# The bias of a norm as four one-element operations, two float16 scratch buffers, and a later weight split

## The chip, the cores and the metric

The kernel runs on one core of one Trainium2 chip. The metric is the device time of one launch in microseconds (us). Before the change the median of 3 runs is 1232.11 us (1230.1 to 1235.2).

The engines of a core work side by side, each through a queue of its own, in order: PE multiplies matrices (PEld loads its stationary operand), DVE does element-wise work on 128 lanes, ACT does activations, copies and sums along a row, POOL does element-wise work in SBUF, and SP issues the DMAs. SBUF is the working memory, PSUM holds what PE writes.

## The reference

Eight batches of 4224 positions with 192 channels. First a dynamic convolution, in which each position and each of 8 heads has its own 7 taps, passed through a softmax. Then, with its output as x, a Fourier mixing, a normalisation and a two-layer network:

```
w = softmax(weight_gen, axis=-1)                    # (8, 4224, 8 heads, 7 taps)
x[b,s,h] = sum_k w[b,s,h,k] * x_pad[b, s+k, h]      # 24 channels to a head
u   = x + real(fft(fft(x, axis=seq), axis=channel))
un  = (u - mean(u)) / sqrt(var(u) + 1e-6)           # over the 192 channels
out = u + relu(un @ w_ch1) @ w_ch2                  # 192 -> 768 -> 192
```

The weights w_ch1 and w_ch2 arrive as 64-bit words. The kernel turns them into 32-bit floats on DVE.

## The kernel before, in words

A batch is 4224 = 128 x 33 positions: 128 partitions and 33 rows of 192 channels. The 33 rows are worked in nine groups, g = 0 to 7 with four rows and g = 8 with one. Per batch b there are these steps:

- conv(b): the softmax of the taps (L271 to L277), and then for each group the products of taps and inputs on DVE (`pr`, L389), which POOL adds up seven to a sum (`u`, L398). POOL folds the sum (`sm`, L410 and L412), PE transforms it along 128 positions (`pg`, L417), ACT and DVE combine the result (L422 to L427), and it goes to DRAM (`g_d`). In batch 0 some sums are made on PE (`pa`), and in batch 1 the products of the first two groups are made on POOL (L387).
- transform(b): `g` is read back, PE transforms it along the 33 rows (`pp`, L456), ACT copies it to `pq`.
- mix(b, g): PE transforms a group along the channels (`eo`, L485); DVE combines (L491, L492) and adds to `u` (L494, L495).
- norm(b, g): the mean and the variance of each of the group's T = 4 rows (one for g = 8). In five early groups ("quick") DVE computes them (L515, L516). In all others ACT sums a row (L521) and the squares of its deviation (L525). Both of these activations write their full result to a tile `junk` that nobody reads; only the accumulated sum is kept, in `st`. Then `rs[:,0]` = 1/sqrt(var + eps) by a square root on ACT (L527) and a reciprocal on DVE (L528), and the bias `rs[:,1]` = -mean * rs[:,0] on DVE in one operation on all T columns (L529). ACT applies scale and bias row by row (`un`, L532), and copies the result to float16 (`hl`, L536). POOL (DVE in the quick groups) computes the float16 remainder (L538, L540), and a DMA transposes both into `ht` (L543).
- mlp(n), n counting the groups of all batches: PE computes `ph` from `ht` and the high and low float16 halves of the first weights (30 matmuls, L568). ACT applies the relu (L574, L578), DVE computes the remainder of the float16 rounding (L579), and PE multiplies group n-1 with the second weights (`po`, L595). DVE scales this and adds it to `u` (L602), and a DMA writes it out.

The second weights exist in two forms. The first nine groups (`F32_GROUPS = 9`, all of batch 0) use the 32-bit `w2f`; all later ones use the float16 halves `w2h` and `w2l` and the scale `isc`. `split_w2` makes the halves: a largest exponent over all of `w2f` on DVE (L174, L175, L177), spread over the partitions by two small matmuls on PE into `ph` banks (L180, L183) with DVE work between them (L181, L184, L186, L188), then three L213, one L255 and three L214 on DVE. Before the change it is emitted at the very start of `rest()`, the stream that also carries conv(1), and may stand no earlier than behind the first matmul group of mlp(0).

The order on each engine is not written out by hand. The steps are generators with a start and an end place; `run()` interleaves them by place, and the framework then orders the instructions of each engine by its own estimate of their times and of when their inputs are ready. `issue_after` and `behind` set the earliest place of a piece. A change of one instruction's kind can therefore move others.

A tile from a pool with `bufs=1` is one buffer that each new use waits for; with `bufs=2` two uses can overlap.

Of the kernel before, what the change touches and what calls it, by code (L numbers as in the profile page):

```python
# [10 lines left out]
F16 = mybir.dt.float16  # L11
F32 = mybir.dt.float32
I32 = mybir.dt.int32
AF = mybir.ActivationFunctionType
ALU = mybir.AluOpType
# [4 lines left out]
P = 128  # L20
# [9 lines left out]
QUICK = 3  # L30
EARLY = 7.4
HELD = 7.0
PP_AT = 4.4
MIX_STEP = 0.8
PE_SUMS = {(0, 0), (0, 1), (0, 3), (0, 5), (0, 7)}
# [51 lines left out]
def tile_dynconv_fnet_mlp(  # L87
# [12 lines left out]
    nc = tc.nc  # L100
    B, D = x.shape[0], x.shape[3]
# [9 lines left out]
    sb = ctx.enter_context(tc.tile_pool(name="sb", bufs=2))  # L111
# [361 lines left out]
    last_product, last_fold, last_gt, last_g2, last_pp = {}, {}, {}, {}, {}  # L473
# [3 lines left out]
    def mix(b, g):  # L477

        u = us[b, g]
        J = 2 if g < NC else 1  # L480
        eo = pst("fft", 2, [P, 2, 2, DH], F32, f"eo_{b}_{g}")
        for e in range(2):
            for j in range(J):
                r = 2 * g + 1 + j if g < NC else 0
                nc.tensor.matmul(eo[:, e, j, :], lhsT=pq[0:DH, e, r, r:r + P], rhs=cs_sb[:, e, :],  # L485
                                 start=True, stop=True)
                yield 0.1 * (J * e + j + 1)
        if g < NC:
            ot = sb.tile([P, 2, DH], F32, tag="ot", name=f"ot_{b}_{g}", bufs=2)
            nc.scalar.copy(ot, eo[:, 1])  # L490
            nc.vector.tensor_tensor(out=eo[:, 1, ::-1, :], in0=eo[:, 0], in1=ot, op=ALU.subtract)  # L491
            nc.vector.tensor_tensor(out=eo[:, 0], in0=eo[:, 0], in1=ot, op=ALU.add)  # L492
            sv = eo.rearrange("p s j d -> p (s j) d")
            nc.vector.tensor_tensor(out=u[:, :, 0:DH], in0=u[:, :, 0:DH], in1=sv, op=ALU.add)  # L494
            nc.vector.tensor_tensor(out=u[:, :, DH:D], in0=u[:, :, DH:D], in1=sv[:, ::-1, DH - 2:0:-1], op=ALU.add)  # L495
        else:
            low, high = u[:, 0, 0:DH], u[:, 0, DH:D]
            for e, op in ((0, ALU.add), (1, ALU.subtract)):
                nc.vector.tensor_tensor(out=low, in0=low, in1=eo[:, e, 0], op=ALU.add)
                nc.vector.tensor_tensor(out=high, in0=high, in1=eo[:, e, 0, DH - 2:0:-1], op=op)  # L500
        yield 2.0

    def norm(b, g):

        T = min(4, N2 - 4 * g)
        u = uv = us[b, g]
        st = sb.tile([P, 4, 2], F32, tag="st", name=f"st_{b}_{g}", bufs=2)
        rs = sb.tile([P, 3, 4], F32, tag="rs", name=f"rs_{b}_{g}", bufs=2)
        junk = sb.tile([P, D], F32, tag="junk", name=f"junk_{b}_{g}", bufs=1)
        un = sb.tile([P, 4, D], F32, tag="un", name=f"un_{b}_{g}", bufs=1)  # L510
        quick = NG * b + g < QUICK or (b == 1 and g < 2)
        if quick:
            bn = sb.tile([P, 4, 6], F32, tag="bn", name=f"bn_{b}_{g}", bufs=2)
            for t in range(T):
                nc.vector.bn_stats(out=bn[:, t, :], in_=uv[:, t, :])  # L515
                last_bn[b, g] = nc.vector.bn_aggr(out=st[:, t, :], in_=bn[:, t, :])  # L516
            nc.scalar.activation(rs[:, 0, 0:T], st[:, 0:T, 1], AF.Sqrt, bias=eps_t)
            neg = -1.0
        else:
            for t in range(T):  # L520
                nc.scalar.activation(junk, uv[:, t, :], AF.Identity, accum_out=st[:, t, 0:1])  # L521
            neg = -1.0 / D
            nc.scalar.mul(rs[:, 2, 0:T], st[:, 0:T, 0], neg)
            for t in range(T):
                nc.scalar.activation(junk, uv[:, t, :], AF.Square, bias=rs[:, 2, t:t + 1],  # L525
                                     accum_out=st[:, t, 1:2])
            nc.scalar.activation(rs[:, 0, 0:T], st[:, 0:T, 1], AF.Sqrt, bias=eps_t, scale=1.0 / D)  # L527
        nc.vector.reciprocal(out=rs[:, 0, 0:T], in_=rs[:, 0, 0:T])  # L528
        nc.vector.scalar_tensor_tensor(out=rs[:, 1, 0:T], in0=st[:, 0:T, 0], scalar=neg, in1=rs[:, 0, 0:T],  # L529
                                       op0=ALU.mult, op1=ALU.mult)  # L530
        for t in range(T):
            nc.scalar.activation(un[:, t, :], uv[:, t, :], AF.Identity,  # L532
                                 bias=rs[:, 1, t:t + 1], scale=rs[:, 0, t:t + 1])
        yield 0.5
        hl = sb.tile([P, 4, 2 * D], F16, tag="hl", name=f"hl_{b}_{g}", bufs=2)
        nc.scalar.copy(hl[:, 0:T, 0:D], un[:, 0:T, :])  # L536
        lo_eng = nc.vector if quick else nc.gpsimd
        lo_eng.tensor_tensor(out=hl[:, 0:T, 2 * P:3 * P], in0=un[:, 0:T, 0:P],  # L538
                                in1=hl[:, 0:T, 0:P], op=ALU.subtract)
        last_lo[NG * b + g] = lo_eng.tensor_tensor(out=hl[:, 0:T, D:2 * P], in0=un[:, 0:T, P:D],  # L540
                                in1=hl[:, 0:T, P:D], op=ALU.subtract)
        ht = sb.tile([P, 4, 3, P], F16, tag="ht", name=f"ht_{b}_{g}", bufs=3)
        nc.sync.dma_start(ht[:, 0:T].rearrange("p t q m -> p (t q) m"),  # L543
                          hl[:, 0:T, :].rearrange("p t d -> p (t d)"), transpose=True)
        state[b, g] = (us.pop((b, g)), ht)
        yield 2.0
# [65 lines left out]
    def add(start, end, gen):  # L612
        streams.append([start, start, end, len(streams), gen])
# [13 lines left out]
    def behind(ins, gen):  # L627

        while True:
            with tc.issue_after(ins):  # L630
                at = next(gen, None)
            if at is None:
                return
            yield at

    def next_conv(b):
        yield from behind((last_gt if b == 2 else last_product)[b - 1].ins, conv(b))

    last_word, last_split, last_lo, last_bn, last_ph, scales = [], [], {}, {}, {}, []
# [4 lines left out]
    def queue(ins, *calls):  # L644
        with tc.issue_after(ins):
            for f, arg in calls:
                f(arg)
# [4 lines left out]
    conv1 = conv(1)  # L652
# [4 lines left out]
    for g in range(QUICK):  # L657
        add(0.0, 1.0, behind((last_word if g else last_split)[-1].ins, mix(0, g)))
        run()
        add(0.0, 1.0, norm(0, g))  # L660
        run()
        queue(last_bn[0, g].ins, (prep_w2, g))
# [1 line left out]
        queue(last_lo[QUICK - 1].ins, (prep_w2, i))  # L664

    def rest():
        with tc.issue_after(last_ph[0].ins):
            queue(last_lo[QUICK - 1].ins, (split_w2, None))
        yield 0.0
        yield from behind(last_ph[0].ins, behind(last_lo[QUICK - 1].ins, behind(last_g2[0].ins, conv1)))  # L670

    def held_mlp(n):
        gen = mlp(n)
        for at in gen:
            yield at
            if n + at >= HELD:
                break
        yield from behind(last_pp[1].ins, gen)

    for n in range(total + 1):  # L680
        add(n, n + 1.0, held_mlp(n) if n == int(HELD) else mlp(n))
    free_at = 1.0
    for b in range(B):
        t0 = NG * b
        pp_at, mix_at, step = (NG - HELD + 0.6, NG - HELD, 0.6) if b == 1 else (PP_AT, 3.0, MIX_STEP)
        if b > 0:
            add(free_at, t0 - pp_at, next_conv(b) if b > 1 else rest())
            add(t0 - pp_at, t0 - mix_at, transform(b))
            free_at = t0 - pp_at
        for g in range(NG):  # L690
            if b > 0 or g >= QUICK:
                at = t0 - mix_at + step * g
                add(at, at + step, mix(b, g))
                add(max(at + step, t0 + g - 2.0), t0 + g - 1.0, norm(b, g))
# [38 lines left out]
```

## Time and profile before

| | |
|---|---|
| median of 3 runs | 1232.11 us |
| the profiled execution, its own time | 1232.47 us |
| its span from the first to the last instruction | 1230.7 us |
| mean granted clock of PE | 0.963 |
| busy: PE, DVE, POOL, ACT | 1098.7, 1059.0, 867.8, 784.9 us |
| L529 (the bias), 72 instructions on DVE | 70.3 us, shortest 144 ns, median 540 ns, longest 5158 ns |
| L521 and L525 (`junk`), 488 on ACT, with their accumulator reads | 198.5 and 92.6 us |

Times in the profile are those of one execution. A busy time is the time in which an instruction of that engine was under way, waiting inside an instruction included. Rows of a view by windows give start and end of the window, its length, and then the busy time of each engine with the number of its instructions, the granted clock of PE as a share of full speed, the busy share of the DMA engines and GB/s. In a timeline a row gives start, duration, engine, line, operation and tiles; in the view by source line a row gives the count, and the shortest, median and longest duration in ns.

### The profile page before, as it was taken

To read this page: it belongs to the slowest core of one execution; us is meant where nothing else is said; L and a number is where in the kernel's file an instruction comes from. 1 tells how busy PE (TensorE), PEld (TensorE's weight loads), DVE (VectorE), ACT (ScalarE), POOL (GpSimd) and SP (SyncE) were. 2 spreads that over 40 slices of the span, in tenths; PEclk is the share of its full clock that TensorE was granted. 3 is DMA by queue.
4 is the path that set the end of the run, shared out by engine and by line. 5 is a ranking of instruction groups with operands and counts; after the bars stand their busy time and mean duration, and the time that the engine had idled before them with its cause. 6 is when DMAs were issued, how large, how long until landed. Compare 5 with 4: busy or idle time off the path is not lost.

```text
span 1230.7 us, 23500 instructions
## 1 busy us (share of the span) xinstructions
PE 1098.7 (89%) x8382; PEld 826.1 (67%) x8382; DVE 1059.0 (86%) x1849; ACT 784.9 (64%) x2353; POOL 867.8 (71%) x686
## 2 busy tenths in 40 slices
PE   5765698998899949999898989998999999999998
PEld 3435466777666827677577766787677776777777
DVE  7999899589999999999998999999989997355543
ACT  1015775263795578858785589657984589479822
POOL 4869478859895989699877988698959898002100
PEclk9986699999999969999999999999999999999999
DMA  8234124722366144633374145623453123512221
GB/s 306 84 109 144 26 59 106 196 77 69 100 170 139 61 97 98 178 95 94 83 190 116 49 110 154 158 66 99 125 134 91 53 68 78 129 43 69 57 64 43
DMA packets 156502, 128.71 MB, mean 105 GB/s; under 512 B 108571, under 2 KB 133088, under 8 KB 156384
## 3 DMA queue, kind: packets, MB, share of 16 engines
q1 hardware_dynamic: 156384, 127.21, 38.4%
q8 instruction: 66, 1.08, 0.4%
q14 instruction: 52, 0.43, 0.1%
HBM read 61.46 MB, written 39.37 MB: 82 GB/s over the span
## 4 chain that ended last, share of the span: by engine, by line
DVE 40%; PE 39%; ACT 7%; DMA 6%; issue 5%; POOL 2%; SPq 1%; DVEq 0%; ACTq 0%; POOLq 0%
PE ph L568 16%; PE po L595 14%; DVE pr L389 14%; DVE hh L579 6%; PE pp L456 5%; DVE rs L529 4%; DMA g<-g_d 2%; DVE u L602 2%; DVE u L389 2%; DMA g_d<-gt 2%; DVE u L494 2%; DVE u L495 2%; PE pg L417 1%; ACT hh L578 1%; PE eo L485 1%
## 5 line engine op out<-in xcount | busy, mean ns | idle before, releaser
L398 POOL TENSOR_TENSOR u<-u,pr 128x768 f32<-128x768 f32 (+1 forms) x395 | 654.8, 1681 | 92.9 <-DVE pr L389 78.3
L568 PE MATMUL ph<-ht,w1h 128*128 128x512 f16 (+1 forms) x1296 | 400.9, 366 | 28.8 <-DVE hh L579 13.5
L595 PE MATMUL po<-w2h,hh 128*128 128x192 f16 x2772 | 398.5, 247 | 11.8 <-DVE u L602 8.9
L595 PEld LDWEIGHTS <-hh 128*128 128x128 f16 x4158 | 356.4, 98 | 73.4 <-issue 13.1
L389 DVE TENSOR_TENSOR pr<-x_sb,wp 128x768 f32<-128x768 f32 (+1 forms) x420 | 357.1, 875 | 12.1 <-POOL u L398 8.1
L595 PE MATMUL po<-w2l,hh 128*128 128x192 f16 x1386 | 336.3, 247 | 0.0
L579 DVE SCALAR_TENSOR_TENSOR hh<-ph,hh 128x512 f16<-128x512 f32 (+1 forms) x378 | 238.5, 639 | 107.3 <-ACT hh L578 106.2
L568 PE MATMUL ph<-ht,w1l 128*128 128x512 f16 (+1 forms) x864 | 312.8, 366 | 0.0
L578 ACT ACTIVATE hh<-ph 128x512 f16<-128x512 f32 (+1 forms) x378 | 207.6, 554 | 125.9 <-PE ph L568 125.0
L538 POOL TENSOR_TENSOR hl<-un,hl 128x512 f16<-128x512 f32 (+1 forms) x67 | 72.7, 1085 | 190.1 <-ACT hl L536 126.6
L568 PEld LDWEIGHTS <-w1h 128*128 128x128 f16 x1296 | 127.2, 100 | 97.6 <-issue 5.8
L532 ACT ACTIVATE un<-u,rs 128x192 f32<-128x192 f32 x264 | 123.6, 537 | 60.1 <-DVE rs L529 52.1
L568 PEld LDWEIGHTS <-w1l 128*128 128x128 f16 x864 | 85.4, 99 | 85.4 <-issue 36.3
L525 ACT ACTIVATE junk<-u,rs 128x192 f32<-128x192 f32 x244 | 110.6, 453 | 4.6
L521 ACT ACTIVATE junk<-u 128x192 f32<-128x192 f32 x244 | 87.9, 360 | 23.1 <-DVE u L495 18.3
L485 PE MATMUL eo<-cs_sb,pq 97*128 97x97 f32 x544 | 82.7, 286 | 21.8 <-DVE u L495 20.6
L485 PEld LDWEIGHTS eo<-cs_sb,pq 97*128 97x128 f32 x544 | 77.4, 203 | 29.0 <-issue 12.7
L460 ACT COPY pq<-pp 97x204 f32<-97x204 f32 (+1 forms) x96 | 46.4, 484 | 65.2 <-PE pp L456 63.2
L595 PE MATMUL po<-w2f,hh 128*128 128x192 f32 x396 | 72.9, 330 | 3.3 <-DVE u L602 2.9
L602 DVE SCALAR_TENSOR_TENSOR u<-po,isc,u 128x384 f32<-128x384 f32 (+1 forms) x119 | 68.5, 596 | 7.9 <-PE po L595 7.5
L417 PE MATMUL pg<-sm,f_sb 128*128 128x192 f32 x256 | 56.4, 345 | 21.1 <-POOL sm L412 13.6
L595 PEld LDWEIGHTS po<-w2f,hh 128*128 128x128 f32 x396 | 66.5, 191 | 9.2 <-DVE u L602 3.7
(101 smaller groups left out, 1331.2 us busy)
## 6 DMA issues: line engine op xcount, KB each, us to landing
out_dram<-u SPq DMA_DIRECT2D x64, 384.0 KB
x_sb<-in_x_dram SPq DMA_DIRECT2D x48, 384.0 KB
g<-g_d SPq DMA_DIRECT2D x40, 336.0 KB
x_sb<-in_x_dram SPq DMA_DIRECT2D x8, 864.0 KB
g_d<-gt SPq DMA_DIRECT2D x32, 195.0 KB
g_d<-gt SPq DMA_DIRECT2D x32, 189.0 KB
w<-in_weight_gen_dram SPq DMA_DIRECT2D x6, 924.0 KB
x_sb<-in_x_dram SPq DMA_DIRECT2D x8, 672.0 KB
```

The lines of the kernel that those rows point to most:

```text
L389: last_product[b] = nc.vector.tensor_tensor(out=dst, in0=rows, in1=wk, op=ALU.mult)
L398: adder.tensor_tensor(out=u, in0=u, in1=pr, op=ALU.add)
L485: nc.tensor.matmul(eo[:, e, j, :], lhsT=pq[0:DH, e, r, r:r + P], rhs=cs_sb[:, e, :], start=True, stop=True)
L521: nc.scalar.activation(junk, uv[:, t, :], AF.Identity, accum_out=st[:, t, 0:1])
L525: nc.scalar.activation(junk, uv[:, t, :], AF.Square, bias=rs[:, 2, t:t + 1], accum_out=st[:, t, 1:2])
L532: nc.scalar.activation(un[:, t, :], uv[:, t, :], AF.Identity, bias=rs[:, 1, t:t + 1], scale=rs[:, 0, t:t + 1])
L538: lo_eng.tensor_tensor(out=hl[:, 0:T, 2 * P:3 * P], in0=un[:, 0:T, 0:P], in1=hl[:, 0:T, 0:P], op=ALU.subtract)
L568: last_ph[n] = nc.tensor.matmul(ph[:, 0:T], lhsT=wt[:, cs_], rhs=ht[:, 0:T, blk], start=(i == 0), stop=(i == len(terms) - 1))
L578: nc.scalar.activation(a[:, 0:T], ph[:, 0:T], AF.Relu)
L579: nc.vector.scalar_tensor_tensor(out=l[:, 0:T], in0=ph[:, 0:T], scalar=0.0, in1=a[:, 0:T], op0=ALU.max, op1=ALU.subtract)
L595: nc.tensor.matmul(po[jj][:, s, :], lhsT=hx[:, t], rhs=wx[:, c2, :], start=(c2 == 0 and i == 0), stop=(c2 == NH - 1 and i == nt - 1))
L602: nc.vector.scalar_tensor_tensor(out=lt, in0=po[jj][:, 0:m], scalar=scales[0][:, 1:2] if NG * lb + lg < F32_GROUPS else isc, in1=lt, op0=A ...
```

## The change

Three things. (1) The bias of the norm, one SCALAR_TENSOR_TENSOR on 128 x T elements, becomes T operations TENSOR_SCALAR on 128 x 1 elements: the mean is the only streamed tensor, and 1/sqrt comes in as a scalar per partition. The arithmetic is the same. (2) `junk` becomes float16 in two buffers, of the same bytes together as the one float32 buffer. (3) `split_w2` leaves the start of `rest()` and gets a stream of its own, `late_split()`, at place 6.0, not before the last matmul of mlp(5) and not before the latest product of conv(1) emitted by then.

```diff
+SPLIT = 5
...
     # in norm(b, g)
-        junk = sb.tile([P, D], F32, tag="junk", name=f"junk_{b}_{g}", bufs=1)
+        junk = sb.tile([P, D], F16, tag="junk", name=f"junk_{b}_{g}", bufs=2)
...
-        nc.vector.scalar_tensor_tensor(out=rs[:, 1, 0:T], in0=st[:, 0:T, 0], scalar=neg, in1=rs[:, 0, 0:T],
-                                       op0=ALU.mult, op1=ALU.mult)
+        for t in range(T):
+            nc.vector.tensor_scalar(out=rs[:, 1, t:t + 1], in0=st[:, t, 0:1], scalar1=rs[:, 0, t:t + 1],
+                                    scalar2=neg, op0=ALU.mult, op1=ALU.mult)
...
     def rest():
-        with tc.issue_after(last_ph[0].ins):
-            queue(last_lo[QUICK - 1].ins, (split_w2, None))
+        yield from behind(last_ph[0].ins, behind(last_lo[QUICK - 1].ins, behind(last_g2[0].ins, conv1)))
+
+    def late_split():
         yield 0.0
-        yield from behind(last_ph[0].ins, behind(last_lo[QUICK - 1].ins, behind(last_g2[0].ins, conv1)))
+        with tc.issue_after(last_ph[SPLIT].ins):
+            queue(last_product[1].ins, (split_w2, None))
+        yield 1.0
...
+    add(SPLIT + 1.0, SPLIT + 1.5, late_split())
```

The changed program has more instructions on DVE alone: 264 TENSOR_SCALAR stand for 72 SCALAR_TENSOR_TENSOR. All other instructions are the same on every engine, but their order differs in many places. Three of them follow, before and then changed. In the changed kernel the line numbers from L34 on are one higher, and from L532 on two.

The first place is DVE in the norms of groups 3 and 4 of batch 0, where the second softmax of conv(1) and the first step of `split_w2` (`ex_w20` to `ex_w22`, `mx_w2`) stand:

```order
L528 RECIPROCAL rs_0_3_991<-rs_0_3_991 128x4
L272 TENSOR_TENSOR w_1_624<-w_1_624,wp_1_623 128x1344
L529 SCALAR_TENSOR_TENSOR rs_0_3_991<-st_0_3_990,rs_0_3_991 128x4
L275 TENSOR_REDUCE wp_1_623<-w_1_624 128x192
L276 TENSOR_SCALAR wp_1_623<-wp_1_623 128x192
L277 RECIPROCAL wp_1_623<-wp_1_623 128x192
L174 TENSOR_SCALAR ex_w20_1013<-w2f_87 128x384
L174 TENSOR_SCALAR ex_w21_1016<-w2f_87 128x384
L174 TENSOR_SCALAR ex_w22_1019<-w2f_87 128x384
L528 RECIPROCAL rs_0_4_1151<-rs_0_4_1151 128x4
```

```order
L529 RECIPROCAL rs_0_3_1000<-rs_0_3_1000 128x4
L273 TENSOR_TENSOR w_1_624<-w_1_624,wp_1_623 128x1344
L531 TENSOR_SCALAR rs_0_3_1000<-st_0_3_999,rs_0_3_1000 128x1 x4
L529 RECIPROCAL rs_0_4_1134<-rs_0_4_1134 128x4
L531 TENSOR_SCALAR rs_0_4_1134<-st_0_4_1133,rs_0_4_1134 128x1 x4
L276 TENSOR_REDUCE wp_1_623<-w_1_624 128x192
L277 TENSOR_SCALAR wp_1_623<-wp_1_623 128x192
L278 RECIPROCAL wp_1_623<-wp_1_623 128x192
L349 TENSOR_TENSOR wp_1_623<-w_1_624,wp_1_623 128x224
L390 TENSOR_TENSOR u_1_2_1191<-x_sb_66,wp_1_623 128x768
```

The steps of the split are gone from here, the bias stands as four operations without anything between them, and the products of conv(1) follow the softmax directly.

The second place is DVE at the end of conv(1), between the last combinations of batch 1 (`gt_1_8`) and the softmax of conv(2):

```order
L426 TENSOR_TENSOR gt_1_8_1860<-pg_1_8_1858,up_1_8_1862 128x95
L427 TENSOR_TENSOR gt_1_8_1860<-pg_1_8_1858,up_1_8_1862 128x95
L271 TENSOR_REDUCE wp_2_1876<-w_2_1877 128x264
L272 TENSOR_TENSOR w_2_1877<-w_2_1877,wp_2_1876 128x1848
L275 TENSOR_REDUCE wp_2_1876<-w_2_1877 128x264
L602 SCALAR_TENSOR_TENSOR u_0_5_397<-po_0_5_0_1780,sc_w1_717,u_0_5_397 128x384
```

```order
L427 TENSOR_TENSOR gt_1_8_1884<-pg_1_8_1882,up_1_8_1886 128x95
L428 TENSOR_TENSOR gt_1_8_1884<-pg_1_8_1882,up_1_8_1886 128x95
L272 TENSOR_REDUCE wp_2_1900<-w_2_1901 128x264
L182 TENSOR_REDUCE m2_w2_1791<-mr_w2_1792 1x1
L273 TENSOR_TENSOR w_2_1901<-w_2_1901,wp_2_1900 128x1848
L604 SCALAR_TENSOR_TENSOR u_0_5_397<-po_0_5_0_1775,sc_w1_717,u_0_5_397 128x384
L604 SCALAR_TENSOR_TENSOR u_0_5_397<-po_0_5_1_1776,sc_w1_717,u_0_5_397 128x384
L185 TENSOR_SCALAR m2_w2_1791<-me_w2_1795 128x1
L187 TENSOR_SCALAR sc_w2_1798<-m2_w2_1791 128x1
L189 TENSOR_SCALAR sc_w2_1798<-m2_w2_1791 128x1
L214 TENSOR_SCALAR w2h_85<-w2f_87,sc_w2_1798 128x384 x3
L256 TENSOR_TENSOR isc_88<-sc_w1_717,sc_w2_1798 128x1
```

The split now stands here; its exponents (L175, L176, L178) lie a few rows ahead and its three L215 three rows behind, around the sum of the softmax (L276). L182 waits for a small matmul of PE, and the softmax of conv(2) is queued behind it.

The third place is ACT at the turn from batch 1 to batch 2, in the norms of the groups (2, 0) and (2, 1):

```order
L527 ACTIVATE rs_2_0_3866<-st_2_0_3865,eps_t_79 128x4
L521 ACTIVATE junk_2_1_4074,st_2_1_4072<-u_2_1_2100 128x192 x4
L523 ACTIVATE rs_2_1_4073<-st_2_1_4072 128x4
L525 ACTIVATE junk_2_1_4074,st_2_1_4072<-u_2_1_2100,rs_2_1_4073 128x192 x2
L422 COPY gt_3_2_4006<-pg_3_2_4003 128x4
L424 COPY up_3_2_4008<-pg_3_2_4003 128x190
L525 ACTIVATE junk_2_1_4074,st_2_1_4072<-u_2_1_2100,rs_2_1_4073 128x192 x2
L527 ACTIVATE rs_2_1_4073<-st_2_1_4072,eps_t_79 128x4
L532 ACTIVATE un_2_0_3868<-u_2_0_1888,rs_2_0_3866 128x192 x4
```

```order
L528 ACTIVATE rs_2_0_3914<-st_2_0_3913,eps_t_79 128x4
L491 COPY ot_2_2_4099<-eo_2_2_4034 128x194
L580 ACTIVATE hh_1_8_3_4235<-ph_1_8_3_4222 128x128
L580 ACTIVATE hh_1_8_4_4266<-ph_1_8_4_4254 128x128
L522 ACTIVATE junk_2_1_4125,st_2_1_4123<-u_2_1_2124 128x192
L534 ACTIVATE un_2_0_3916<-u_2_0_1912,rs_2_0_3914 128x192 x3
L522 ACTIVATE junk_2_1_4125,st_2_1_4123<-u_2_1_2124 128x192
L534 ACTIVATE un_2_0_3916<-u_2_0_1912,rs_2_0_3914 128x192
```

Before, the rows of group (2, 0) are normalised behind all eight sums of group (2, 1); now behind one of them.

## The prediction

> **What bounds the kernel now.** I read the busy times first, then the chain of waits, then both by stages.
>
> ```profile
> PE 1098.7 (89%) x8382; PEld 826.1 (67%) x8382; DVE 1059.0 (86%) x1849; ACT 784.9 (64%) x2353; POOL 867.8 (71%) x686
> DVE 40%; PE 39%; ACT 7%; DMA 6%; issue 5%; POOL 2%; SPq 1%; DVEq 0%; ACTq 0%; POOLq 0%
> PE ph L568 16%; PE po L595 14%; DVE pr L389 14%; DVE hh L579 6%; PE pp L456 5%; DVE rs L529 4%; DMA g<-g_d 2%; DVE u L602 2%; DVE u L389 2%; DMA g_d<-gt 2%; DVE u L494 2%; DVE u L495 2%; PE pg L417 1%; ACT hh L578 1%; PE eo L485 1%
> ```
>
> No engine is full, and the chain is shared by DVE and PE. One entry is out of proportion: L529, a tiny operation on the bias, holds 4% of the chain, about 49 us. By stages (columns: PE, PEld, DVE, ACT, POOL, clock of PE, DMA share, GB/s):
>
> ```profile
> 150.00:180.00 30.00, 27.25 (x150) 19.83 (x149) 29.93 (x51) 25.61 (x81) 20.57 (x16) 1.00 0.24 60
> 180.00:210.00 30.00, 25.21 (x137) 18.39 (x135) 28.92 (x44) 13.91 (x36) 24.93 (x18) 1.00 0.39 96
> 210.00:240.00 30.00, 29.71 (x165) 23.10 (x164) 19.60 (x34) 9.05 (x20) 29.92 (x27) 1.00 0.67 186
> 240.00:270.00 30.00, 28.85 (x199) 23.52 (x198) 21.54 (x27) 17.38 (x41) 10.57 (x8) 1.00 0.38 107
> 270.00:300.00 30.00, 29.09 (x191) 24.00 (x190) 29.16 (x54) 13.67 (x33) 28.92 (x19) 1.00 0.16 46
> 300.00:1050.00 750.00, 687.38 (x5657) 521.88 (x5656) 710.01 (x1228) 550.85 (x1697) 635.50 (x499) 0.97 0.42 108
> 1050.00:1231.00 181.00, 175.63 (x1542) 134.68 (x1540) 84.20 (x170) 107.26 (x316) 15.70 (x20) 1.00 0.25 66
> ```
>
> From 300 to 1050 us DVE is the fullest: idle 40.0 of 750 us, with PE idle 62.6. Behind 1050 us the convolutions are over, DVE is half idle and PE at 97%: this end is PE's alone. In 150 to 300 us PE is idle 9.9 us. So the middle stage decides, and there DVE's time. What L529 does with it:
>
> ```profile
> L529 DVE SCALAR_TENSOR_TENSOR rs<-st,rs x72: 144/540/5158, 110.8 to 1162.4; 128x4 f32<-128x4 f32 x64, 128x1 f32<-128x1 f32 x8
>   ACT un L532: 52.1, 22
> 100.00:300.00 200.00, 9.65 (x11) 0.91 0.35 94
> 300.00:1050.00 750.00, 58.53 (x52) 0.97 0.42 108
> 1050.00:1231.00 181.00, 2.15 (x9) 1.00 0.25 66
> ```
>
> The second row is what waited for it, the last three are its busy time on DVE by stage. One costs 1.13 us in the middle and 0.24 us at the end, where POOL is busy 15.70 of 181 us. So it is not the operation that is slow; something of POOL's holds it. One case, with the chain behind it and PE over the same time:
>
> ```profile
> 434.01 8.93 POOL L398 TENSOR_TENSOR u<-u,pr 128x768 f32<-128x768 f32 x5
> 434.48 1.13 DVE L602 SCALAR_TENSOR_TENSOR u<-po,isc,u 128x384 f32<-128x384 f32 x2
> 437.91 5.05 DVE L529 SCALAR_TENSOR_TENSOR rs<-st,rs 128x4 f32<-128x4 f32 x1
> 443.06 1.86 ACT L532 ACTIVATE un<-u,rs 128x192 f32<-128x192 f32 x4 [4.75 <-DVE rs L529]
> 456.75 5.07 PE ph L568 x15
> 436.00:457.00 21.00, 5.47 (x31) 4.72 (x29) 19.24 (x27) 15.71 (x59) 17.32 (x14) 0.59 0.41 107
> ```
>
> POOL adds five times without a gap up to 442.94; L529 enters at 437.91 and ends at 442.96, with POOL. DVE stands for 5 us, ACT waits for the bias, and PE gets its next `ht` only at 456.75. PE works 5.47 of these 21 us, and its clock falls to a mean of 0.59. L602 ran under the same POOL adds at 0.56 us each: it reads one streamed tensor from SBUF (`u`), a scalar per partition (`isc`), and the other tensor from PSUM. L529 reads two streamed tensors from SBUF. That is the difference that the change removes.
>
> **The bias.** It takes away 72 L529 (70.3 us) and puts 264 operations on one element in their place, each with one streamed tensor and a scalar. The nearest rows are TENSOR_SCALAR on one element, in SBUF, while POOL works in SBUF:
>
> ```profile
> 169.93 1.16 POOL L538 TENSOR_TENSOR hl<-un,hl 128x512 f16<-128x512 f32 x1
> 170.74 0.14 DVE L186 TENSOR_SCALAR sc_w<-m_w 128x1 int32<-128x1 f32 x1
> 170.80 0.14 DVE L188 TENSOR_SCALAR sc_w<-m_w 128x1 int32<-128x1 f32 x1
> 170.86 0.53 DVE L495 TENSOR_TENSOR u<-u,eo 128x380 f32<-128x380 f32 x1
> ```
>
> L186 starts and ends inside L538, lasts 0.14 us, and the next start 0.06 us apart. Four independent ones cost 3 x 0.06 + 0.14 = 0.32 us; if they did not overlap, 4 x 0.14 = 0.56. The rows have constants where the new operation has one scalar from SBUF; L602 above shows that such a scalar doesn't wait. I take 0.32. In the middle stage that is 52 x 0.32 = 16.6 us in place of 58.5: DVE gets back 41.9 us (29.4 by 0.56). From 100 to 300 us, 9.65 - 11 x 0.32 = 6.1 us. At the end 2.15 becomes 2.9, covered by PE.
>
> The Trainium skill speaks against this kind of edit: "VectorE: DVE Perf Modes", section "Rules for kernel authors", says to keep the number of operations low. An estimate by its section on the fixed latency, (58 + 1) cycles at 0.96 GHz or 61 ns for each of 192 more, is 12 us more on DVE. By that alone, without any waiting, the edit would lose; the trace agrees on the 60 ns, and the sum above has them in it.
>
> How much of 41.9 us reaches the end? If DVE keeps its 40.0 us of idleness, the stage takes 710.0 - 41.9 + 40.0 = 708 us. If PE comes to the 97% of the last stage, 687.4 / 0.97 = 709 us. Both say 41 us, but both engines would have to be that full at once, and they feed each other. I take three quarters, 31 us; half (21) and all of PE's idle time (62.6) are the bounds.
>
> What is late next shows in the waits:
>
> ```profile
> POOL hl L538 <- ACT hl L536: 126.6, 20, 47.6
> PE ph L568 <- DVE hh L579: 13.5, 18, 2.3
> PE po L595 <- DVE u L602: 11.8, 12, 2.2
> ```
>
> PE's largest ones are for banks that DVE empties late (L579, L602). POOL stands in its queue at L538 until ACT has `hl`, which hangs on the bias; that shrinks too.
>
> **The split.** Moved are 18 instructions on DVE and two small matmuls on PE with their `ph` banks; no DMA, nothing of SP or POOL. DVE's share between 150 and 186 us:
>
> ```profile
> L214 DVE SCALAR_TENSOR_TENSOR w2l<-w2f,sc_w,w2h 128x384 f16<-128x384 f32 x3 | 3.3, 1139 | 0.0
> L213 DVE TENSOR_SCALAR w2h<-w2f,sc_w 128x384 f16<-128x384 f32 x3 | 2.7, 959 | 0.0
> L255 DVE TENSOR_TENSOR isc<-sc_w,sc_w 128x1 f32<-128x1 f32 x1 | 1.8, 1770 | 0.0
> L175 DVE TENSOR_REDUCE mx_w<-ex_w 128x1 f32<-128x384 int32 x3 | 1.5, 538 | 0.0
> L174 DVE TENSOR_SCALAR ex_w<-w2f 128x384 int32<-128x384 int32 x3 | 0.9, 348 | 0.0
> ```
>
> With five more small ones at 0.14 us, as L186, that is 10.9 us. They leave a stage where DVE is full (58.9 of 60 us to 210) and come back at the end of conv(1), where DVE is idle 18.9 of 60 us (210 to 270), since POOL is full to 240 and then the softmax waits for ACT. The new wait is that of L182 for PE: behind it on DVE stands the softmax of conv(2), and for that all products of batch 2 wait, and POOL. The gain is at most PE's 9.9 us of idleness from 150 to 300; the loss, if none of the idle time takes the split up, 10.9 us. POOL, full to 240, lets conv(1) end only a little earlier, so I take half of the gain, 5 us, with the 6.1 us of early L529 in it.
>
> **The scratch buffers.** Float16 instead of float32 output on ACT:
>
> ```profile
> L578 ACT ACTIVATE hh<-ph 128x512 f16<-128x512 f32 x336 | 196.8, 590 | 117.4 <-PE ph L568 116.5
> L574 ACT ACTIVATE hh<-ph 128x512 f32<-128x512 f32 x48 | 27.9, 592 | 28.7 <-PE ph L568 28.7
> ```
>
> 590 against 592 ns: nothing. All uses of `junk` are on ACT, in order, so no engine waits for the buffer; the second one only lets the order interleave two norms. The third place of the order shows `un` of group (2, 0) behind one sum of the next norm rather than eight:
>
> ```profile
> L525 ACT ACTIVATE junk<-u,rs 128x192 f32<-128x192 f32 x244 | 110.6, 453 | 4.6
> L521 ACT ACTIVATE junk<-u 128x192 f32<-128x192 f32 x244 | 87.9, 360 | 23.1 <-DVE u L495 18.3
> ```
>
> The seven sums are 4 x 0.45 + 3 x 0.36 = 2.9 us of ACT, gained there and lost for the next norm; they lie in a hole that the bias makes anyway, so I add nothing. Without that cover one such turn to a batch would be worth 2.9 us either way.
>
> **Sum.** Against the profiled 1232.47 us, 0.4 above the median: 1232.5 - 31 - 5 = 1196.5, and by the median 1196 us.
>
> **Rivals.**
>
> The holes close almost wholly: PE runs the middle stage nearly as it does here,
>
> ```profile
> 1100.00:1150.00 50.00, 50.00 (x444) 38.59 (x443) 30.98 (x75) 47.87 (x168) 9.95 (x12) 1.00 0.30 67
> ```
>
> at 99%, and the start gives 8. 687.4 / 0.99 = 694, 56 less than 750: about 1168 us. For it: the hole at 436 us follows directly from one L529, at half the clock. Against it: three engines share the work evenly, and DMAs, 6% of the chain, stop PE whatever DVE does.
>
> The relief goes into other waits: only the worst hole (15.5 us without PE work in 21) shrinks, by some 12 us, and elsewhere POOL (635.5 of 750 us) or ACT's queue holds the work: 1220 us. For it: POOL's 126.6 us at L538. Against it: DVE is the fullest, and stands still while it waits.
>
> Slower: the new operations wait for POOL too, each of the four by itself. L213 above is a TENSOR_SCALAR with a scalar from SBUF, and it does wait:
>
> ```profile
> L213 DVE TENSOR_SCALAR w2h<-w2f,sc_w x3: 408/1147/1321, 175.1 to 177.4; 128x384 f16<-128x384 f32 x3
> ```
>
> From its shortest to its median are 0.74 us. Four times 0.14 + 0.74 are 3.5 us a norm in place of 1.13, 125 us more in the middle stage; with three quarters of it, 1326 us. It decides from a wait of 0.14 us each on (4 x 0.28 = 1.13). Against it stands L186, on one element under POOL, without a wait.
>
> The Trainium skill has a rule for this rival: "SBUF — State Buffer", section "Who interferes with whom", lets TENSOR_SCALAR enter modes that use two ports and then lock POOL out or wait for it. L213 agrees with it at 384 elements, L186 does not at one.
>
> The change does not do what it says: the time in L529 is another wait, for L528's result or for ACT, that the new operations inherit. Then only 5 us at most change: 1230 us. Against it: L529 ended with POOL's run, 0.02 us behind.
>
> **How the numbers follow.** Forecast (1184 to 1210) 0.50; holes close (below 1184) 0.20; relief lost (1210 to 1226) 0.18; inherited wait 0.06; waits for POOL, or an order that turns out worse, 0.06. A measurement tells 0.5%, 6 us, from no change. So faster 0.88, same 0.06, slower 0.06. The range 1172 to 1222 leaves out the outer parts of the second and third case and the last two.
>
> **What would show it.** The new bias operations: median 0.14 us, none over 0.3; ACT's wait for the bias from 52.1 to under 10 us; PE at 95 to 96% there, without half-clock stretches after 300; the split between 230 and 260 us with DVE elsewhere unchanged. Wrong: bias operations that end with POOL's adds, PE holes of the old length, or the softmax of conv(2) over 10 us later.

## The result, and the profile after

The changed kernel takes 1192.5 us (median of 4 runs, 1192.1 to 1194.5) against 1231.6 us before: a ratio of 0.968, 95% interval 0.966 to 0.971. In a second comparison it was 0.965 (0.963 to 0.967). That is 39 to 43 us, 3.2 to 3.5%; predicted were 36 us.

The profiled execution took 1194.5 us. From the page of the changed kernel, the busy times, and then by stages (columns as before: PE, PEld, DVE, ACT, POOL, clock, DMA share, GB/s). The middle stage is cut at 1011 us, since the last transform starts that much earlier:

```profile
PE 1095.0 (92%) x8382; PEld 827.0 (69%) x8382; DVE 1027.1 (86%) x2041; ACT 779.2 (65%) x2353; POOL 867.8 (73%) x686
```

```profile
180.00:210.00 30.00, 29.47 (x163) 22.60 (x162) 24.76 (x41) 14.35 (x40) 30.00 (x23) 1.00 0.39 109
210.00:240.00 30.00, 26.64 (x133) 21.16 (x132) 20.13 (x37) 6.53 (x15) 24.33 (x22) 0.90 0.73 199
240.00:270.00 30.00, 29.24 (x198) 23.06 (x198) 25.88 (x38) 17.86 (x41) 12.48 (x7) 0.99 0.28 80
300.00:1011.00 711.00, 678.80 (x5633) 517.40 (x5633) 672.71 (x1361) 545.86 (x1694) 631.52 (x496) 0.98 0.43 114
1011.00:1193.00 182.00, 178.24 (x1560) 136.64 (x1558) 89.14 (x197) 106.66 (x318) 16.58 (x22) 1.00 0.25 66
```

PE's and POOL's work is what it was. The middle stage is 711 us long instead of 750; PE is busy in 95.5% of it (91.7% before) and DVE in 94.6%. The last stage has not changed.

Where the time went shows in the starts of the transforms. The matmuls of transform(1) and transform(7), changed kernel (L457) and then the kernel before (L456); behind the colon stand the durations in ns, then the first and last start in us:

```profile
L457 PE MATMUL pp<-te_sb,g x44: 224/251/330, 249.2 to 261.8; 102*97 102x102 f32 x42, 68*97 68x68 f32 x2
L457 PE MATMUL pp<-te_sb,g x44: 222/251/254, 1021.1 to 1043.4; 102*97 102x102 f32 x42, 68*97 68x68 f32 x2
```

```profile
L456 PE MATMUL pp<-te_sb,g x44: 224/251/330, 252.2 to 262.8; 102*97 102x102 f32 x42, 68*97 68x68 f32 x2
L456 PE MATMUL pp<-te_sb,g x44: 223/251/300, 1059.9 to 1081.4; 102*97 102x102 f32 x42, 68*97 68x68 f32 x2
```

Transform(1) starts 3.0 us earlier and transform(7) 38.8: 35.8 us are gained in the six batches between, 6 us each, and nothing behind.

The bias by source line, what waited for it, its busy time on DVE in the middle stage, and one case under POOL's adds, all of the changed kernel:

```profile
L531 DVE TENSOR_SCALAR rs<-st,rs x264: 195/205/216, 112.7 to 1118.2; 128x1 f32<-128x1 f32 x132
  ACT un L534: 12.2, 10
300.00:1011.00 711.00, 27.48 (x190) 0.98 0.43 114
416.27 8.92 POOL L399 TENSOR_TENSOR u<-u,pr 128x768 f32<-128x768 f32 x5
422.99 0.57 DVE L531 TENSOR_SCALAR rs<-st,rs 128x1 f32<-128x1 f32 x4
```

The longest of 264 took 0.216 us; before, the longest of 72 took 5.158. The four run through in 0.57 us while POOL adds without a gap from 416.27 to 425.19. It is the same norm of group (2, 0) that stood for 5.05 us before.

### The profile page after: what moved, and what is told of

The parts are those of the page before. It is cut to its first block, busy times and chain, and to the rows that moved or that the text cites. A ratio compares the mean times of both kernels' runs of the same rounds, so it can differ in the third digit from the quotient of the medians.

```text
span 1192.7 us, 23723 instructions
## 1 busy us (share of the span) xinstructions
PE 1095.0 (92%) x8382; PEld 827.0 (69%) x8382; DVE 1027.1 (86%) x2041; ACT 779.2 (65%) x2353; POOL 867.8 (73%) x686
## 5 line engine op out<-in xcount | busy, mean ns | idle before, releaser
L399 POOL TENSOR_TENSOR u<-u,pr 128x768 f32<-128x768 f32 (+1 forms) x395 | 655.3, 1679 | 69.5 <-DVE pr L390 62.6
L534 ACT ACTIVATE un<-u,rs 128x192 f32<-128x192 f32 x264 | 125.6, 537 | 19.8 <-DVE rs L531 12.2
L526 ACT ACTIVATE junk<-u,rs 128x192 f16<-128x192 f32 x244 | 110.4, 453 | 3.5
L522 ACT ACTIVATE junk<-u 128x192 f16<-128x192 f32 x244 | 87.8, 360 | 16.6 <-DVE u L496 12.1
L486 PE MATMUL eo<-cs_sb,pq 97*128 97x97 f32 x544 | 79.8, 282 | 17.8 <-DVE u L496 13.3
L486 PEld LDWEIGHTS eo<-cs_sb,pq 97*128 97x128 f32 x544 | 73.8, 198 | 24.4 <-issue 13.1
L395 PE MATMUL pa<-pr,ident 128*128 128x384 f32 x140 | 54.6, 540 | 20.5 <-DVE pr L390 17.8
```

What stands on the lines that cost most here:

```text
L399: adder.tensor_tensor(out=u, in0=u, in1=pr, op=ALU.add)
```

## The experiments

Differences to the changed kernel are between ratios to the kernel before, times 1232 us, with 0.968 for the changed kernel. Every one of these programs gets an order of its own from the framework, on all engines, so that a few us of each difference may be the order's.

**The parts alone.** Four kernels: the kernel before with one part each, and the changed kernel without the split's move.

```diff
 e1  -nc.vector.scalar_tensor_tensor(out=rs[:, 1, 0:T], ...)
     +for t in range(T): nc.vector.tensor_scalar(out=rs[:, 1, t:t + 1], ...)
 e2  -junk = sb.tile([P, D], F32, ..., bufs=1)
     +junk = sb.tile([P, D], F16, ..., bufs=2)
 e3  +late_split(), and split_w2 taken out of rest()
 e4  e1 and e2 together
```

> The kernel before with the bias as four one-element TENSOR_SCALAR, nothing else changed. If the bias's wait for POOL's adds is what costs (my theory), this alone gives nearly all of the 39 us: 31 to 38 us off 1232. If the gain came from the split or from the order that it brought, this gives under 15 us.

> The kernel before with float16 junk in two buffers, nothing else changed. All of junk is on ACT, in order: 0 us, with what a new order adds, within 4 us either way. If the second buffer lets ACT work off norms earlier and that matters, over 6 us faster.

> The kernel before with the split of the second weights moved, nothing else changed. My sum: 2 to 5 us faster (the first 3 us show at the start of transform(1), the split runs without waits at 0.42 and 0.61 us). The rival, that the split only moves from one full stage to another: 0, or up to 8 us slower.

> The changed kernel with the split left where it was (bias and junk changed). If the parts add up: 3 us slower than the changed kernel, 1195 to 1197 us. If the split's place matters more than its 3 us at the start, over 1200 us.

| run | median, us | ratio to before | 95% interval |
|---|---|---|---|
| e1, the bias alone | 1200.4 | 0.971 | 0.968 to 0.974 |
| e2, the scratch buffers alone | 1238.6 | 1.003 | 1.000 to 1.005 |
| e3, the split alone | 1233.2 | 0.998 | 0.995 to 1.001 |
| e4, bias and buffers, no split | 1194.3 | 0.966 | 0.963 to 0.969 |

The kernel before had a median of 1235.0 us beside these four. The bias alone gives 36 of the 39 us. The buffers alone are 3 us slower at the edge of the interval, the split alone can't be told from nothing, and without the split the change is as fast as with it. The split's 3 us at the start do not show in the time. e4 is 6 us faster than e1 in the same rounds (1192.4 to 1197.4 against 1198.5 to 1201.6 us): with the bias changed, the kernel with the buffers is the faster one. Whether the buffers do this or the order that comes with them is not shown.

**What makes the bias wait.** Two controls on the changed kernel. The first keeps four operations on one element, but streams both operands from SBUF. The second keeps one streamed operand, but takes four elements at once; it leaves out the scales of rows 2 to 4 and uses that of the first row for all.

```diff
 e5  -nc.vector.tensor_scalar(out=rs[:, 1, t:t + 1], in0=st[:, t, 0:1], scalar1=rs[:, 0, t:t + 1], scalar2=neg, ...)
     +nc.vector.scalar_tensor_tensor(out=rs[:, 1, t:t + 1], in0=st[:, t, 0:1], scalar=neg, in1=rs[:, 0, t:t + 1], ...)
 e6  -for t in range(T): nc.vector.tensor_scalar(out=rs[:, 1, t:t + 1], ...)
     +nc.vector.tensor_scalar(out=rs[:, 1, 0:T], in0=st[:, 0:T, 0], scalar1=rs[:, 0, 0:1], scalar2=neg, ...)
```

> The changed kernel with each of the four one-element operations as a SCALAR_TENSOR_TENSOR that streams both mean and 1/sqrt from SBUF, as before, instead of taking 1/sqrt as a scalar. Same number and size of operations. If two streams from SBUF are what waits for POOL (my theory), the waits come back: the longest bias operation over 2 us, mean over 0.4 us, and the time 1225 to 1245 us. If it was the one larger operation, or the wait for the reciprocal, that cost, the four stay near 0.2 us and the time near 1193.

> The changed kernel with one TENSOR_SCALAR on all T columns, with the scale of the first row for all of them: the bias of rows 2 to 4 of a group is computed with the wrong row's scale, all else is done. One streamed tensor, but four elements. If a TENSOR_SCALAR of an even size waits for POOL as the 384-element ones of the split do (the Trainium skill's rule), the longest is over 2 us and the time 1220 to 1240 us. If only a second streamed tensor waits, all are at 0.2 us and the time 1180 to 1193 us, DVE having 0.37 us a norm less to do.

The bias in the first control by source line, what waited for it, and one case with POOL beside it:

```profile
L531 DVE SCALAR_TENSOR_TENSOR rs<-st,rs x264: 125/151/6183, 110.5 to 1195.4; 128x1 f32<-128x1 f32 x132
  ACT un L534: 68.2, 58
446.13 2.17 DVE L531 SCALAR_TENSOR_TENSOR rs<-st,rs 128x1 f32<-128x1 f32 x4
446.34 3.72 POOL L399 TENSOR_TENSOR u<-u,pr 128x768 f32<-128x768 f32 x2
```

And in the second:

```profile
L530 DVE TENSOR_SCALAR rs<-st,rs x72: 202/324/7112, 110.8 to 1155.4; 128x4 f32<-128x4 f32 x64, 128x1 f32<-128x1 f32 x8
448.96 1.80 DVE L530 TENSOR_SCALAR rs<-st,rs 128x4 f32<-128x4 f32 x1
445.38 7.13 POOL L399 TENSOR_TENSOR u<-u,pr 128x768 f32<-128x768 f32 x4
```

e5 takes 1273.0 us, ratio 1.030 (1.026 to 1.034): 76 us slower than the changed kernel, 3% slower than before, and slower than expected. Number and size of the operations are the same; 1/sqrt is a second stream in place of a scalar, which makes the operation a SCALAR_TENSOR_TENSOR. The waits are back, at up to 6.2 us, with four chances to wait in a norm instead of one. So the number of operations is not what helped. That it is the stream from SBUF and not the kind of operation shows below, where the same kind with one stream from PSUM does not wait.

e6 takes 1231.5 us, 0.997 (0.994 to 1.000): the time of the kernel before, with one streamed operand. Here my theory was too narrow: one operation TENSOR_SCALAR on four elements waits as well, up to 7.1 us. The Trainium skill says so ("SBUF — State Buffer", section "Who interferes with whom": TENSOR_SCALAR can use both ports if its operands meet certain conditions, and can then contend with GpSimd); this run agrees with it at four elements. In the changed kernel none of the 264 operations on one element waits, though POOL is busy for 631.52 of the middle stage's 711 us. Both halves of the edit are needed: the scalar operand, and the single element.

**What a stop of DVE costs.** Three runs on the changed kernel vary DVE's time. One adds four more operations like the bias's behind it. One adds one operation as before the change, which waits for POOL, behind it. One takes the bias off DVE and gives it to ACT.

```diff
 e7   +spare = sb.tile([P, 4], F32, tag="spare", ..., bufs=2)
      +for t in range(T): nc.vector.tensor_scalar(out=spare[:, t:t + 1], in0=st[:, t, 0:1], scalar1=rs[:, 0, t:t + 1], ...)
 e9   +nc.vector.scalar_tensor_tensor(out=spare[:, 0:T], in0=st[:, 0:T, 0], scalar=neg, in1=rs[:, 0, 0:T], ...)
 e10  -nc.vector.tensor_scalar(out=rs[:, 1, t:t + 1], ...)
      +nc.scalar.mul(rs[:, 1, t:t + 1], rs[:, 2, t:t + 1], rs[:, 0, t:t + 1])
```

> The changed kernel with four more one-element operations of the same kind behind the four, written to a tile that nobody reads: 38 us more on DVE, none of it a wait for POOL and none ahead of ACT's use of the bias. If DVE's time as such sets the middle stage (my sum, three quarters of it), 25 to 32 us slower, 1218 to 1225 us. If the gain came mostly from the ends of single long waits, under 12 us slower.

> The changed kernel, and behind the four operations one more SCALAR_TENSOR_TENSOR with two streams from SBUF, as before the change, into a tile that nobody reads. DVE stands for POOL as it did before, but ACT has its bias already. By the dose of the run with doubled operations (38 us of DVE gave 15 to 17) some 70 us more on DVE would give 30 us, 1222 us, if standing is as cheap as working. If a single long stop costs more than its length, since ACT, PE and PE's clock fall behind it whoever waits for the bias, 1235 to 1265 us. If it was ACT's wait for the bias that made the holes, under 1210 us.

> The changed kernel with the bias made on ACT (not in the quick groups): four one-element multiplications of the negative mean by 1/sqrt, in place of the four on DVE. DVE gets back another 36 us, which by the dose of the doubled run is worth 14 us: 1178 us, if ACT's 244 more small operations (about 0.2 us each, 50 us of ACT at 65%) are hidden. If ACT's queue is as tight as DVE's, 1190 to 1205 us.

The added operations in e7, and in e9 with their busy time from 300 to 1050 us:

```profile
L535 DVE TENSOR_SCALAR spare<-st,rs x264: 197/203/209, 112.5 to 1137.9; 128x1 f32<-128x1 f32 x132
```

```profile
L534 DVE SCALAR_TENSOR_TENSOR spare<-st,rs x72: 146/472/8343, 111.3 to 1153.8; 128x4 f32<-128x4 f32 x64, 128x1 f32<-128x1 f32 x8
  ACT un L537: 0.9, 1
300.00:1050.00 750.00, 48.03 (x52) 0.97 0.42 108
```

| run | added on DVE over the span | ratio (interval) | to the changed kernel |
|---|---|---|---|
| e7, work behind the bias | 38.1 us | 0.981 (0.976 to 0.985) | +15 us |
| e9, waits behind the bias | 56.9 us | 0.996 (0.994 to 0.999) | +35 us |
| e6, waits as the bias | 72.1 for 38.2 us: 33.9 | 0.997 (0.994 to 1.000) | +35 us |
| e10, the bias on ACT | 36 us less | 0.965 (0.962 to 0.969) | -4 us |

e7 and e9 both lie between their expectations. By these runs, one of each kind and each with its own order, a us of plain work on DVE costs 0.4 us of the whole, one of waiting behind the bias 0.6, and one of waiting ahead of ACT's use of the bias about 1.0. (With 0.965 for the changed kernel, its second ratio, they are 0.5, 0.7 and 1.2.) e9 rules out that ACT's wait alone made the loss: ACT waited there for these operations in one case (0.9 us), and the time was still back within 0.4% of the kernel before. That the rest of e6's price is ACT's wait is an inference; the orders of the two differ.

**Can DVE give more?** e10 seemed 4 us faster, within its interval, so it ran again beside the changed kernel.

> The changed kernel itself, on the same chip and in the same rounds as the next run, so that the two can be compared: ratio to the kernel before 0.966 to 0.971.

> The bias on ACT once more, beside the changed kernel. If DVE's time still sets the middle stage, 36 us less of it must show: at least 8 us faster than the changed kernel. If PE at over 95% of that stage is the limit by now, within 5 us of it.

They came out at 1193.1 and 1194.9 us, 0.965 (0.963 to 0.967) and 0.966 (0.963 to 0.968): no difference. The bias on ACT, and then the stretch from the start of transform(1) to that of transform(7), which holds nearly the same work in both: first of the changed kernel as it ran beside it (e11), then of the kernel with the bias on ACT (e12).

```profile
L536 ACT ACTIVATE rs<-rs x244: 277/283/348, 144.8 to 1123.7; 128x1 f32<-128x1 f32 x122
```

```profile
243.70:1017.80 774.10, 739.65 (x6051) 564.58 (x6050) 726.54 (x1453) 577.95 (x1772) 674.43 (x524) 0.98 0.42 111
```

```profile
253.10:1021.40 768.30, 732.62 (x6040) 563.72 (x6041) 701.96 (x1261) 599.99 (x1961) 673.70 (x524) 0.99 0.43 112
```

DVE does 24.6 us less in the stretch and ACT 22.0 more, and the stretch is 5.8 us shorter, about a quarter of what DVE gave up; PE is busy in 95% of it. In the first traces of the two kernels it is 764.9 against 771.9 us. But the stretch also starts later, at 250.9 and 253.1 us against 249.2 and 243.7, and by the medians nothing of the gain is left. Why it starts later is open. So taking this time off DVE makes the kernel no faster, though adding some still costs.

**One operation without the wait.** A kernel in which ACT leaves the sums for the mean in spare columns of the PSUM bank that holds the taps (`wp`). The bias can then be one SCALAR_TENSOR_TENSOR again, with one stream from SBUF. This was meant to beat the changed kernel.

```diff
 e8  +sm1 = wbanks[max(wbanks)][:, lo:lo + T]
     -nc.scalar.activation(junk, uv[:, t, :], AF.Identity, accum_out=st[:, t, 0:1])
     +nc.scalar.activation(junk, uv[:, t, :], AF.Identity, accum_out=sm1[:, t:t + 1])
     ...
     -for t in range(T): nc.vector.tensor_scalar(out=rs[:, 1, t:t + 1], ...)
     +nc.vector.scalar_tensor_tensor(out=rs[:, 1, 0:T], in0=sm1, scalar=neg, in1=rs[:, 0, 0:T], ...)
```

> The changed kernel, with the sum for the mean accumulated into spare columns of a PSUM bank, and the bias again one SCALAR_TENSOR_TENSOR on all T columns, one stream from PSUM and one from SBUF. By my theory it doesn't wait for POOL: 0.15 to 0.25 us each, 0.57 to 0.2 us a norm, 24 us less on DVE, and the time 1175 to 1190 us. If a SCALAR_TENSOR_TENSOR waits as such, the long ones are back and the time is over 1220 us.

The bias by source line, and from the waits of this kernel the ones that grew:

```profile
L535 DVE SCALAR_TENSOR_TENSOR rs<-wp,rs x67: 149/161/164, 142.2 to 1275.3; 128x4 f32<-128x4 f32 x59, 128x1 f32<-128x1 f32 x8
POOL u L399 <- DVE pr L390: 233.6, 50, 19.4
PE ph L578 <- DMA ht<-hl: 106.3, 24, 12.2
ACT junk L526 <- DVE pr L390: 67.8, 32, 9.0
```

It took 1324.1 us, 1.071 (1.067 to 1.076). As an operation it does what the theory says: the same kind on the same four elements, with one stream from PSUM, took 0.164 us at most, with POOL busy for 66% of the span. But ACT's sums now stand 67.8 us for DVE's products, which read the taps in the same bank, and everything behind is late. That the framework guards the bank as a whole is likely, and was not tested. No kernel here beats the changed one.

## Why the prediction was right, point by point

- **What bounds.** DVE's stops in the middle stage decided: right. 35.8 of the 38.8 us came there, and the bias alone gives 36 us.
- **The price of the new bias, 0.32 us a norm.** Mis-sized: it is 0.57 (the row at 422.99), the upper end that I had put at 0.56. One takes 0.205 us against 0.14 for L186 (none took over 0.3, as said), and four need 0.57, so that they start 0.12 us apart and not 0.06. L186 has constants where these read a scalar per partition; that this is the reason was not tested by itself. DVE got back 58.53 - 27.48 = 31.0 us in the middle stage, not 41.9.
- **Three quarters of it reach the end.** This step failed the other way: from 31.0 us it would have made 23, and 35.8 were measured. The two errors cancel in the 31 us of the sum, and that is luck. Before and then changed, from the start of transform(1) to that of transform(7), which holds nearly the same work in both:

```profile
252.20:1059.90 807.70, 741.45 (x6046) 565.70 (x6044) 759.23 (x1309) 579.90 (x1771) 674.61 (x524) 0.98 0.41 106
249.20:1021.10 771.90, 737.54 (x6051) 563.97 (x6050) 726.01 (x1453) 577.90 (x1772) 674.64 (x524) 0.98 0.42 111
```

  DVE's busy time fell by 33.2 us, of which the bias is 32.4 (60.99 to 28.61), and its idle time from 48.5 to 45.9: all of the bias's time reached the end, and a little more. So the cruder estimate in the same place, that DVE keeps its idleness, was the better one: 807.7 - 32.4 = 775.3 us, and 771.9 were measured. That its 708 us for the stage from 300 us on come so near to the measured 711 is luck in part: with the 31.0 us that came free it gives 719, and some of DVE's other work now lies outside the two ends of that stage. One rate for all of DVE's time does not hold either: e7, e9 and e6 show 0.4 to about 1.0 us for a us, and e12 shows nothing gained from 24.6 us less.
- **The split, 5 us.** Not shown. It runs where it was expected, and without waits:

```profile
248.00 1.08 DVE L214 TENSOR_SCALAR w2h<-w2f,sc_w 128x384 f16<-128x384 f32 x3
249.00 0.15 DVE L256 TENSOR_TENSOR isc<-sc_w,sc_w 128x1 f32<-128x1 f32 x1
251.06 1.67 DVE L215 SCALAR_TENSOR_TENSOR w2l<-w2f,sc_w,w2h 128x384 f16<-128x384 f32 x3
```

  These seven took 7.8 us before and 2.9 now; POOL is busy for only 12.48 of 30 us there. DVE's load from 180 to 210 us fell from 28.92 to 24.76, and POOL went to 30.00 of 30: as feared, POOL passed little of it on. The 3 us in the trace's transform(1) are no sign of it: it starts at 252.2 us before, at 249.2 and 243.7 in two executions of the changed kernel, and at 257.8 with the split alone (e3). No run shows the 5 us of the sum.
- **The scratch buffers, nothing.** Right alone: 1.003. Beside the bias it is open (e4 against e1, 6 us). Each sum on ACT takes what it took, but with two buffers they overlap more: ACT is on `junk` for 239.06 us in place of 243.57. The buffers alone have that too (238.61) and gain nothing.
- **What is late next.** Half right. PE's waits for banks that DVE empties fell (L602: 11.8 to 9.5 us; L579: 13.5 to 6.4 us), but POOL's wait for `hl` did not:

```profile
POOL hl L540 <- ACT hl L538: 129.4, 18, 44.9
PE po L597 <- DVE u L604: 9.5, 10, 1.8
PE ph L570 <- DVE hh L581: 6.4, 7, 1.7
```

- **The signs.** ACT's wait for the bias fell from 52.1 to 12.2 us, not below 10; PE came to 95.5%, as said. The hole at 436 us is now 430 to 440, at a clock of 0.66, so that stretches at half clock remain:

```profile
430.00:440.00 10.00, 5.75 (x22) 2.75 (x23) 9.83 (x26) 9.49 (x36) 10.00 (x10) 0.66 0.71 202
```

- **The rivals.** The holes closed by half: PE is idle for 32.2 us of the middle stage, against 62.6 before, and busy in 95.5% of it, not 99%. The relief did not go into POOL's wait for `hl`, which is as long as before while the time fell. That the wait is inherited fell with e1 and e5; besides, all 37 of L529 that took over 0.5 us ended within 0.1 us of the end of an instruction of POOL. That the new operations wait for POOL fell for one element, but e6 shows how near it was: one operation on four elements would have given 1231 us. The Trainium skill's rule against many small operations ("VectorE: DVE Perf Modes", "Rules for kernel authors") does not decide here, where four operations are faster than one that waits; but they are not free: four more in a norm cost about 15 us (e7).

## What to carry to other kernels

Look at the spread of a small operation's duration and not at its size: a shortest of 144 ns with a longest of 5158 names a wait inside the instruction, and the same line in a stage where the other engine is idle confirms it. When DVE and POOL share a stage, feed small per-partition factors as scalar operands, one element at a time, rather than as a second tensor; and measure whether a wider form still passes. Where two engines stand at about 95%, as DVE and PE here, relief for one alone may bring nothing: 24.6 us off DVE left the whole as it was (e12).

## What the runs showed of the hardware that I had not expected

- TENSOR_SCALAR on 128x4 in SBUF waits for POOL's adds, up to 7.1 us; on 128x1 the longest of 264 took 0.216 us in the changed kernel.
- DVE can wait through several of POOL's instructions, not one: up to 8.3 us (e9), with single adds at 1.8 us.
- A TENSOR_SCALAR of one element took about 0.14 us with constants (L186) and 0.205 us with a scalar per partition from SBUF (L531). That the scalar is the reason was not tested.
- A SCALAR_TENSOR_TENSOR with one stream from PSUM and one from SBUF doesn't wait for POOL: 0.149 to 0.164 us in 67 cases.
